# Dummy products at TensorE's waits, two queries on ScalarE and 90 instead of 87 VectorE key tiles in a planned attention layer

## The chip, the cores and the metric

The kernel runs on one core of a Trainium2 chip. Its time is device microseconds from start to end of one execution; the kernel before was run three times (347.79, 348.11 and 348.26 us; median 348.11). The core's engines are TensorE (PE in the profile; PEld are its weight loads), VectorE (DVE), ScalarE (ACT), GpSimd (POOL) and SyncE (SP), which issues most of the DMAs. Each engine runs its own list of instructions in order; semaphores hold them together.

## The reference: what is computed

A transformer layer on x of 2048 rows by 448 columns, in bf16: layer norm, attention with 16 query heads of 28 dimensions that share one key and one value head, a residual, a second layer norm, and then a routed MLP that only 8 of the 2048 rows pass through.

```
q = layernorm(x) @ wq   # 16 heads of 28
k = layernorm(x) @ wk ; v = layernorm(x) @ wv          # one head each
h = x + softmax(q k^T / sqrt(28)) v @ wo
y = layernorm(h)
r = y @ w_r ; idx = the 8 rows with the largest r
upd[idx] = (silu(y[idx] @ w_gate) * (y[idx] @ w_up)) @ w_down * sigmoid(r[idx])
out = h + y + upd
```

## The kernel before, in words

**Tiles.** The 2048 rows are 16 row tiles of 128. Attention goes by 16 query blocks (128 rows, 16 heads, so 2048 queries) against 16 key tiles of 128. For one block and one key tile TensorE makes the scores in four strips of 128x512 (`scores`, matmuls at L823). The strips' exponentials are made by one of two engines:

- an *A tile* on ScalarE: two ACTIVATE instructions of 128x1024 (L888; L874 for the early tiles below), and one group of four probability-times-value products (`pv_op`, L853, P and Vs);
- a *D tile* on VectorE: four TENSOR_SCALAR instructions of 128x512 that clip the score and use its integer bits as a bf16 number (L915, tile Y). GpSimd makes two shifted copies of the four strips with 64-bit adds (L926, tile Yc), and the three are multiplied with three differently scaled value tiles, so a D tile has three groups of products (L853, Y and Yc) where an A tile has one.

`_ND` says how many of each block's 16 key tiles are D tiles: 87 of the 256 in all. `_EARLY` names three A tiles of block 1 whose strips are made while block 0 runs; their results wait in the space of the MLP weights (`wg_sb`, `wu_sb`).

**Head.** The key and value of all rows are needed before block 0 can finish. The rows are taken in seven groups (`group`: tiles 0; 1; 2,3; 4,5; 6,7; 8 to 11; 12 to 15). A group's rows go through VectorE statistics (L724, L726), Ln and Exp on ScalarE (L728, L730), the normalization (on VectorE at L737 or L746, for tiles 1 and 2 on ScalarE at L742), TensorE transposes (L757), a VectorE copy (L762), the key product with `wk_rep` (an L628 matmul), the key's writing by VectorE (L772) and the value (L785). A key tile is kept twice, in two placings of its partitions (`K[:, 0]` and `K[:, 1]`, r = 0 and 1); strips 0 and 2 read the first, strips 1 and 3 the second. VectorE writes both, except for the groups in `_KD`, where two DMAs copy the second from the first. `q_project` makes a block's queries (16 matmuls of 128x128); VectorE adds a bias while it copies them from PSUM (L806), only the first half of block 0's is done by ScalarE (L803).

**Body.** Per block there are also a copy of the accumulator (L953), the sums' way through DRAM to their reciprocals (L959, `Rb`), the scaling (L966), the output projection `out_proj`, the residual (L996), statistics (L998, L999), the product with w_r (L1001) and, a few tiles at a time, the second norm `ln2` (L1012 to L1034).

**Tail.** For tiles 0 to 13 the best 8 rows of each are found early (`stage1`) and fetched by an indirect DMA (L1127, tile `wqx`/`cand`, norms at L1137 to L1146). `tail` then finishes block 15, norms row tile 15 (`last_rows`, L1041 to L1060), finds the best 8 of all (L1200, L1201), multiplies them with the MLP weights, fetches their rows of the output by an indirect DMA (L1256, tile `base`), adds, and writes them back (L1267).

**What sets the order.** Nothing above is emitted in the order written. Each instruction is an operation with an engine, a planned duration, reads and writes, and a priority; `_Flow.plan` is a list scheduler that places them one by one and gives every engine its fixed list. The tables `_W`, `_LOOK`, `_WIN`, `_LATE`, `_HOLD`, `TURN`, `MORE` are its rules and costs, in ns. It also gives out the PSUM banks; bank 7 (`ACC`) holds the accumulator. A lock keeps some VectorE operations and GpSimd's apart in the plan.

Of the kernel before, what the change touches and what calls it, by code (L numbers as in the profile page):

```python
# [240 lines left out]
_KD = (1, 2, 4)  # L241
_EARLY = (0, 6, 9)
# [37 lines left out]
class _Flow(_Graph):  # L280
# [7 lines left out]
    TURN = 105.0  # L288
# [225 lines left out]
def _fast(nc, G, sb, ps, psb, flag, scr, rows, A_x, A_wq, A_wk, A_wv, A_wo, B_w_r, B_w_gate, B_w_up, B_w_down, out):  # L514
# [154 lines left out]
    G.op(DV, lambda e: e.memset(idi[:, :], 1.0), 100, writes=["idi"])
# [49 lines left out]
    def group(g):  # L719
# [29 lines left out]
        for a in range(t0, t1, 2):  # L749
# [9 lines left out]
            G.op(PE, [tr(k, ch) for k in range(m) for ch in range(NCH)], m * 4 * (150 if g == 0 else 80),  # L759
                 reads=[("of", a + k) for k in range(m)] + ["ident"], writes=[u.key], take=u)  # L760
# [8 lines left out]
                  for ch in range(NCH)], 4 * (145 if g == 0 else 5 + w / 2.4), reads=[("wkr", r) for r in range(4)] + ["wk_rep"] + [("xnT", t) for t in tl_],  # L769
# [1097 lines left out]
```

## Time and profile before

| | |
|---|---|
| median of three runs | 348.11 us |
| the profiled execution | 348.56 us, its span 346.6 us |
| ScalarE busy | 325.45 us |
| VectorE busy | 319.37 us |
| TensorE busy (modelled ends) | 318.17 us |
| GpSimd busy | 190.76 us |
| ScalarE in 40 to 320 us | 280.00 of 280 us |
| VectorE in 40 to 320 us | 266.13 of 280 us |

The profiled execution's 1.96 us outside the span are not in the trace. A row of the timeline has the start, the time from the first start to the last end, the engine, the line, the operation, what it writes and reads, and how many instructions were merged (x); in brackets the idle time before it and what ended it. A row of the windows has busy time and number (x) of each engine in that stretch.

### The profile page before, as it was taken

How to read it: one execution, taken by the hardware profiler on the slowest of the kernel's cores; microseconds unless marked ns; L12 is line 12 of the kernel's file. 1: busy time of each engine (PE TensorE's matmuls, PEld its weight loads, DVE VectorE, ACT ScalarE, POOL GpSimd, SP SyncE). 2: the span in 40 equal slices, each digit the busy share in tenths (PEclk: the TensorE clock that was granted, in tenths of full speed). 3: DMA queues.
4: the chain of work that ended last, by engine and by line, in shares of the span. 5: the costliest groups of instructions: out<-in, count | busy, mean ns of one | idle time of the engine just before them, and what ended most of it. 6: DMA issues, size and time to landing. Idle time of an engine off the chain costs nothing.

```text
span 346.6 us, 8725 instructions
## 1 busy us (share of the span) xinstructions
PE 318.2 (92%) x3630; PEld 105.2 (30%) x3630; DVE 319.4 (92%) x662; ACT 325.4 (94%) x387; POOL 190.8 (55%) x206
## 2 busy tenths in 40 slices
PE   3889899999999999999999998999999999999974
PEld 2644232323232322323232322323232322222334
DVE  6998997999988999999899899999999899999874
ACT  5599999999999999999999999999999999999850
POOL 8010475666545648667456566576747456775401
PEclk9999999999999999999999999999999999999995
DMA  6510000000020205020020206020101012152210
GB/s 158 138 40 3 0 3 18 20 17 18 5 85 4 84 4 168 27 60 30 8 80 5 84 4 165 4 46 16 33 4 30 7 58 85 42 152 58 60 36 9
DMA packets 18374, 16.18 MB, mean 47 GB/s; under 512 B 6574, under 2 KB 15438, under 8 KB 18330
## 3 DMA queue, kind: packets, MB, share of 16 engines
q1 hardware_dynamic: 16826, 15.01, 15.5%
q8 instruction: 29, 0.48, 0.6%
q10 hardware_dynamic: 1392, 0.45, 0.6%
q0 software_dynamic: 112, 0.12, 0.1%
q14 instruction: 15, 0.12, 0.1%
HBM read 11.78 MB, written 3.71 MB: 45 GB/s over the span
## 4 chain that ended last, share of the span: by engine, by line
ACT 83%; DVE 9%; DMA 3%; PE 3%; issue 0%; POOLq 0%; POOL 0%; ACTq 0%; DVEq 0%
ACT P L888 80%; DVE Y L915 4%; PE ps L628 2%; DMA wqx<-in_A_wq_dram 1%; ACT wg_sb L874 1%; DMA wqx<-n_rows,cidx 1%; DVE bn L724 1%; PE ps L823 1%; DMA cidx<-gidx 1%; ACT wu_sb L874 1%; DVE K L772 0%; ACT wqx L711 0%; DVE Q L806 0%; PE ps L757 0%; DVE gidx L1123 0%
## 5 line engine op out<-in xcount | busy, mean ns | idle before, releaser
L888 ACT ACTIVATE P<-ps 128x1024 bf16<-128x1024 f32 x332 | 306.8, 1287 | 0.0
L926 POOL INT64_ADD Yc<-Y x174 | 178.5, 1037 | 127.7 <-DVE Y L915 112.3
L915 DVE TENSOR_SCALAR Y<-ps 128x512 int16<-128x512 f32 x348 | 220.0, 683 | 12.0 <-PE ps L823 11.3
L823 PE MATMUL ps<-Q,K 32*128 32x512 bf16 (+1 forms) x1024 | 147.1, 386 | 14.1 <-ACT P L888 10.8
L823 PEld LDWEIGHTS ps<-Q,K 32*128 32x128 bf16 (+1 forms) x1024 | 37.7, 91 | 142.9 <-ACT P L888 122.1
L853 PE MATMUL ps<-Yc,Vs 128*32 128x512 bf16 x696 | 63.9, 385 | 0.0
L853 PE MATMUL ps<-P,Vs 128*32 128x512 bf16 x664 | 59.4, 387 | 0.0
L853 PE MATMUL ps<-Y,Vs 128*32 128x512 bf16 x348 | 34.2, 384 | 0.2 <-DVE Ot L953 0.2
L853 PEld LDWEIGHTS ps<-P,Vs 128*32 128x32 bf16 x664 | 14.1, 93 | 28.3 <-issue 26.2
L853 PEld LDWEIGHTS ps<-Yc,Vs 128*32 128x32 bf16 x696 | 15.7, 94 | 21.5 <-issue 15.8
L628 PE MATMUL ps<-xnT,wqx 112*128 112x128 bf16 x256 | 21.6, 229 | 0.0
L628 PE MATMUL ps<-wo_pad,On 128*32 128x448 bf16 (+1 forms) x244 | 18.1, 358 | 1.2 <-DVE Y L915 0.6
L628 PEld LDWEIGHTS ps<-xnT,wqx 112*128 112x128 bf16 x256 | 15.6, 102 | 7.7 <-issue 4.8
L806 DVE TENSOR_SCALAR Q<-ps,qone 128x512 bf16<-128x512 f32 (+1 forms) x16 | 11.6, 727 | 1.0 <-PE ps L628 0.9
L853 PEld LDWEIGHTS ps<-Y,Vs 128*32 128x32 bf16 x348 | 9.1, 94 | 9.3 <-issue 7.4
L966 DVE TENSOR_TENSOR On<-Ot,Rb 128x512 bf16<-128x512 f32 x15 | 11.0, 734 | 0.5 <-DMA Rb<-l_scr 0.5
L757 PE MATMUL ps<-ident,of 128*112 128x128 bf16 x64 | 6.3, 248 | 5.5 <-DVE of L737 5.5
L996 DVE TENSOR_TENSOR of<-ps,x_sb 128x448 bf16<-128x448 f32 x15 | 9.3, 619 | 1.1 <-PE ps L628 1.1
L953 DVE COPY Ot<-ps 128x512 f32<-128x512 f32 x15 | 10.3, 685 | 0.0
L724 DVE BATCH_NORM_STATS2 bn<-x_sb 128x6 f32<-128x448 bf16 x16 | 9.5, 610 | 0.0
L998 DVE BATCH_NORM_STATS2 bn<-of 128x6 f32<-128x448 bf16 x15 | 9.3, 622 | 0.1
L1001 DVE SCALAR_TENSOR_TENSOR junk<-of,w_rb 128x448 bf16<-128x448 bf16 x14 | 8.5, 611 | 0.0
(169 smaller groups left out, 141.4 us busy)
## 6 DMA issues: line engine op xcount, KB each, us to landing
Rb<-l_scr SPq DMA_DIRECT2D x15, 256.0 KB
out_dram<-of SPq DMA_DIRECT2D x16, 112.0 KB, 2.2
n_rows<-of SPq DMA_DIRECT2D x14, 113.0 KB, 2.4
x_sb<-in_A_x_dram SPq DMA_DIRECT2D x3, 448.0 KB, 4.4
wg_sb<-in_B_w_gate_dram SPq DMA_DIRECT2D x3, 448.0 KB, 6.1
wu_sb<-in_B_w_up_dram SPq DMA_DIRECT2D x3, 448.0 KB, 6.1
xnT<-in_B_w_down_dram SPq DMA_DIRECT2D x3, 448.0 KB, 7.7
wqx<-in_A_wq_dram ACTq DMA_DIRECT2D x1, 392.0 KB, 4.6
```

Of the source, the lines that this page charges most:

```text
L628: return lambda e: e.matmul(o() if callable(o) else o, lhsT=l, rhs=r, start=start, stop=stop)
L724: G.op(DV, lambda e, t=t: e.bn_stats(bn6[:, t, :], x_sb[:, t, :]), 516, reads=[("x", t)], writes=[("bn6", t)], after=[G.last_w[("xnT", 0)] ...
L806: G.op(DV, lambda e, c=c, src=src: e.tensor_scalar(Q[:, b % 3, c[0]:c[1], :], src(), qone[:, 0:1], None, ALU.add), 60 + n * 150, reads=[u. ...
L823: return e.matmul(ps[:, u.b[0] + q, :], lhsT=K[a:a + w, i % 2, j * 128:(j + 1) * 128], rhs=Q[a:a + w, b % 3, :, :].rearrange("p h n -> p ( ...
L853: return e.matmul(ps[32 * i:32 * i + 32, ACC, :], lhsT=Vs[:, v, j, :], rhs=src(i), start=info["first"] == o.idx, stop=info["last"] == o.idx)
L888: G.op(AC, lambda e, u=u, p=p, n=n: e.activation(P[:, p:p + n, :], ps[:, u.b[0]:u.b[0] + n, :], ACT.Exp, bias=EB, scale=OCT), 50.0 + 426.5 ...
L915: G.op(DV, lambda e, u=u, g0=g0: e.tensor_scalar(Y0[:, g0, :].bitcast(I16), ps[:, u.b[0], :], 0.0, TOP - STEP[-1], ALU.max, ALU.min), 599, ...
L926: G.op(PO, lambda e: e.int64_add(Yc[:, c, :, :].rearrange("p a b -> p (a b)").bitcast(I64), Y0[:, 4 * s:4 * s + 4, :].rearrange("p a b -> ...
L953: o = G.op(DV, lambda e: e.tensor_copy(Ot[:, rb, :], ps[:, ACC, :]), 598, reads=[pk(ACC)], writes=[("Ot", rb)], prio=b - 10.0, after=blk[b ...
L966: G.op(DV, lambda e: e.tensor_tensor(On[:, rb, :, :].rearrange("p h n -> p (h n)"), Ot[:, rb, :], Rb[:, rb, :], ALU.mult), 599, reads=[("O ...
L996: G.op(DV, lambda e: e.tensor_tensor(of[:, t, 0:D], hp(), x_sb[:, t, :], ALU.add), 535, reads=[u.key, ("x", t)], writes=[("of", t)], free=u)
L998: G.op(DV, lambda e: e.bn_stats(bn6[:, t, :], of[:, t, 0:D]), 520, reads=[("of", t)], writes=[("bn6", t)])
```

## The change

It has four parts.

**Dummy products.** A helper `fill` puts products of a tile of ones with itself, 128x128x128, into the accumulator's bank, whose first real product overwrites it: 44 at the very start, 8 and 6 after the transposes of groups 0 and 1, 5 after the key product of group 0, 9 after block 0's queries. The planned durations of the first group's products are lowered (transposes 150 to 100 ns, key product 145 to 75, queries 470 and 430 to 235).

**Queries and keys of the head.** The second half of block 0's queries is copied by ScalarE too. The second placing of the keys comes by DMA for groups 3 and 5 instead of 1, 2 and 4. All three early tiles are due at the same place of block 0 (3, 3, 3 for 0, 6, 9). The two masks that GpSimd makes (`tri`, `ident`) carry a planned wait for its first 64-bit add.

**Planned times.** An exp of 128x1024 is planned at 917.4 ns for 903, a score or value group at 226 for 231, and several norm steps likewise; `TURN`, `MORE` and the weights change with them, and the plan gives a new order. `_ND` sums to 90.

**Tail.** The product with w_r of tile 14 no longer waits for its norm: it is made unscaled and multiplied by it afterwards. Tile 14's Ln is put behind the last block's reciprocals, and its two normalizations behind the Exp of tile 15's norm. The count of sums that are in range (`okc`) waits for the last product before the down projection.

```
-_KD = (1, 2, 4)
-_EARLY = (0, 6, 9)
+_KD = (3, 5)
+_EARLY = (3, 3, 3)
-_ND = (2, 7, 6, 3, 7, 7, 6, 5, 5, 7, 6, 5, 4, 5, 6, 6)
+_ND = (2, 6, 7, 4, 6, 6, 5, 7, 6, 6, 5, 6, 7, 5, 6, 6)
-_LOOK = 111.5
+_LOOK = 167.8
-    TURN = 105.0
+    TURN = 92.0
...
+    def fill(n, ns, after):
+        G.op(PE, [mm(ps[:, ACC, 0:128], idi[:, :], idi[:, :], True, True) for _ in range(n)], n * ns, reads=["idi"],
+             writes=[pk(ACC)], after=after, prio=-1999)
+
+    fill(44, 98, ())
...
+            if g == 0:
+                fill(8, 56, [o])
+            elif g == 1:
+                fill(6, 56, [o])
...
         if g == 0:
+            fill(5, 56, [G.last_w[uk.key][0]])
             q_project(0)
+            fill(9, 56, [o for o in G.ops[-8:] if o.eng == PE][-1:])
...
-            if b == 0 and c[0] == 0:
+            if b == 0:
                 G.op(AC, lambda e, c=c, src=src: e.activation(Q[:, 0, c[0]:c[1], :], src(), ACT.Identity, bias=qone[:, 0:1]),
-                     340, reads=[u.key, "qone"], writes=[("Qa", 0)], free=u)
+                     340, reads=[u.key, "qone"], writes=[("Qa" if c[0] == 0 else "Q", 0)], free=u)
...
-                                                           scale=OCT), 50.0 + 426.5 * n,
+                                                           scale=OCT), 64.0 + 426.7 * n,
...
-                G.op(DV, lambda e, t=t: e.scalar_tensor_tensor(junk[:, :], of[:, t, 0:D], st[:, t, 1:2], w_rb[:, :], ALU.mult,
-                                                               ALU.mult, accum_out=st[:, t, 4:5]), 600,
...
+        for o in late15:
+            o.deps[q.idx] = False
...
+        for o in late14:
+            o.deps[q.idx] = False
```

The orders below are what the plan made of it. The first place is TensorE's head. The names: `idi` the tile of ones, `ident,of` the transposes, `wk_rep` the key product, `wqx` the queries, `wv_sb` the value, `Q,K` score strips, `P,Vs` value products of an A tile. Before:

```order
L757 MATMUL ps<-ident,of 112x128 x4
L628 MATMUL ps<-xnT,wk_rep 128x128 x4
L628 MATMUL ps<-xnT,wqx 128x128 x16
L628 MATMUL ps<-wv_sb,xnT 128x28 x4
L757 MATMUL ps<-ident,of 112x128 x4
L823 MATMUL ps<-Q,K 128x512 x2
L628 MATMUL ps<-xnT,wk_rep 128x128 x4
L823 MATMUL ps<-Q,K 128x512 x2
```

After:

```order
L628 MATMUL ps<-idi 128x128 x44
L763 MATMUL ps<-ident,of 112x128 x4
L628 MATMUL ps<-idi 128x128 x8
L628 MATMUL ps<-xnT,wk_rep 128x128 x4
L628 MATMUL ps<-wv_sb,xnT 128x28 x4
L628 MATMUL ps<-idi 128x128 x5
L628 MATMUL ps<-xnT,wqx 128x128 x16
L628 MATMUL ps<-idi 128x128 x9
L835 MATMUL ps<-Q,K 128x512 x4
```

The dummies stand ahead of the first transposes and between the steps of group 0; the first tile's four strips follow the queries directly, ahead of group 1's transposes.

The second place is ScalarE from the queries of block 0 to the tenth exponential (`var`, `rstd` a group's norm; `of` the normalization of tile 1 or 2; `P` and `wg_sb` exponentials). Before:

```order
L742 ACTIVATE of<-x_sb,nb,rstd 128x448
L803 ACTIVATE Q<-ps,qone 128x256
L728 ACTIVATE var<-mv,ebias 128x2
L730 ACTIVATE rstd<-var 128x2
L742 ACTIVATE of<-x_sb,nb,rstd 128x448
L888 ACTIVATE P<-ps 128x1024 x2
L728 ACTIVATE var<-mv,ebias 128x2
L730 ACTIVATE rstd<-var 128x2
L728 ACTIVATE var<-mv,ebias 128x2
L730 ACTIVATE rstd<-var 128x2
L874 ACTIVATE wg_sb<-ps 128x1024 x2
L888 ACTIVATE P<-ps 128x1024 x4
```

After:

```order
L815 ACTIVATE Q<-ps,qone 128x256 x2
L734 ACTIVATE var<-mv,ebias 128x2
L748 ACTIVATE of<-x_sb,nb,rstd 128x448
L736 ACTIVATE rstd<-var 128x2
L900 ACTIVATE P<-ps 128x1024
L748 ACTIVATE of<-x_sb,nb,rstd 128x448
L900 ACTIVATE P<-ps 128x1024 x2
L734 ACTIVATE var<-mv,ebias 128x2 x2
L736 ACTIVATE rstd<-var 128x2 x2
L900 ACTIVATE P<-ps 128x1024 x5
L886 ACTIVATE wg_sb<-ps 128x1024 x2
```

Tile 1's normalization went behind the queries, tile 2's behind the first exponential, and eight exponentials of block 0 now come ahead of the first early tile.

The third place is ScalarE in the tail, from the last block's reciprocals on (`Rb` their Ln and Exp; `st` the norm of one row tile; `cst` that of the fetched rows; `xnT` and `of` a row tile's normalizations). Before:

```order
L1158 ACTIVATE Rb<-Ot 128x256
L1012 ACTIVATE st<-of,ebias 128x1
L1160 ACTIVATE Rb<-Rb 128x256
L1014 ACTIVATE st<-st 128x1
L1137 ACTIVATE cst<-wqx,ebias 112x1
L1139 ACTIVATE cst<-cst 112x1
L1026 ACTIVATE xnT<-of,st 128x448
L1030 ACTIVATE of<-of,st 128x448
L1043 ACTIVATE st<-of,ebias 128x1
L1045 ACTIVATE st<-st 128x1
L1058 ACTIVATE xnT<-ps,st 128x448
L1060 ACTIVATE of<-ps,st 128x448
```

After:

```order
L1171 ACTIVATE Rb<-Ot 128x256
L1173 ACTIVATE Rb<-Rb 128x256
L1025 ACTIVATE st<-of,ebias 128x1
L1027 ACTIVATE st<-st 128x1
L1150 ACTIVATE cst<-wqx,ebias 112x1
L1152 ACTIVATE cst<-cst 112x1
L1054 ACTIVATE st<-of,ebias 128x1
L1056 ACTIVATE st<-st 128x1
L1037 ACTIVATE xnT<-of,st 128x448
L1071 ACTIVATE xnT<-ps,st 128x448
L1073 ACTIVATE of<-ps,st 128x448
L1041 ACTIVATE of<-of,st 128x448
```

Tile 15's norm (Ln and Exp of `st`) moved ahead of tile 14's two normalizations, and stays behind the norm of the fetched rows; tile 14's output normalization is now the last of the four.

More of the change, by code (lines that the diff above doesn't have):

```diff
@@ L758, in tr @@
                                              of[:, a + k, ch * CK + cut(a, ch):(ch + 1) * CK + cut(a, ch)], ident[:, :])
-            G.op(PE, [tr(k, ch) for k in range(m) for ch in range(NCH)], m * 4 * (150 if g == 0 else 80),
-                 reads=[("of", a + k) for k in range(m)] + ["ident"], writes=[u.key], take=u)
+            o = G.op(PE, [tr(k, ch) for k in range(m) for ch in range(NCH)], m * 4 * (100 if g == 0 else 80),
+                     reads=[("of", a + k) for k in range(m)] + ["ident"], writes=[u.key], take=u)
+            if g == 0:
+                fill(8, 56, [o])
+            elif g == 1:
+                fill(6, 56, [o])
             dst = xnT[0:CK, :, a * 128:(a + m) * 128]
@@ L768, in group @@
         G.op(PE, [mm(bank(uk, c=slice(0, w)), wk_rep[0:CK, ch, :], xnT[0:CK, ch, sl], ch == 0, ch == NCH - 1)
-                  for ch in range(NCH)], 4 * (145 if g == 0 else 5 + w / 2.4), reads=[("wkr", r) for r in range(4)] + ["wk_rep"] + [("xnT", t) for t in tl_],
+                  for ch in range(NCH)], 4 * (75 if g == 0 else 5 + w / 2.4), reads=[("wkr", r) for r in range(4)] + ["wk_rep"] + [("xnT", t) for t in tl_],
              writes=[uk.key], take=uk)
@@ L832, in scores @@
             u.half = True
-        o = G.op(PE, [part(q, *p) for q, p in enumerate(parts)] if parts else strip, 231,
+        o = G.op(PE, [part(q, *p) for q, p in enumerate(parts)] if parts else strip, 226,
                  reads=[("Q", b_ % 3) for b_, j_ in need] + [("K", r, j_) for b_, j_ in need for r in range(2) if j_ not in late or r == 0] +
@@ L855, in fn @@
             return run
-        o = G.op(PE, [fn(i) for i in range(4)], 231, form="P", reads=reads + [("V", j), "Vone%d" % v], prio=key,
+        o = G.op(PE, [fn(i) for i in range(4)], 226, form="P", reads=reads + [("V", j), "Vone%d" % v], prio=key,
                  after=[blk[b - 1]["evict"] if b else None])
@@ L971, in _fast @@
     blk14 = []
+    late14 = []
+    late15 = []
     def out_proj(t):
@@ L1011, in ln2 @@
         sv = of[:, sl, D:RW].bitcast(F32)
-        G.op(AC, lambda e: e.activation(st[:, sl, 0], sv[:, :, 1], ACT.Ln, bias=ebias[:, 0:1]), 300,
-             reads=[("stf", t) for t in ts] + ["ebias"], writes=[("st0", t) for t in ts])
-        G.op(AC, lambda e: e.activation(st[:, sl, 1], st[:, sl, 0], ACT.Exp, scale=-0.5), 100, reads=[("st0", t) for t in ts],
+        ln = G.op(AC, lambda e: e.activation(st[:, sl, 0], sv[:, :, 1], ACT.Ln, bias=ebias[:, 0:1]), 175,
+                  reads=[("stf", t) for t in ts] + ["ebias"], writes=[("st0", t) for t in ts])
+        G.op(AC, lambda e: e.activation(st[:, sl, 1], st[:, sl, 0], ACT.Exp, scale=-0.5), 87, reads=[("st0", t) for t in ts],
              writes=[("st1", t) for t in ts])
@@ L1279, in tail @@
                                                                      accum_out=okc[:, n:n + 1]), dvt(w), reads=rd + ["okj"],
-                 writes=["okj", ("okc", n)], prio=900.0 if n == 0 else 1005, lock=True)
+                 writes=["okj", ("okc", n)], prio=900.0 if n == 0 else 1005, lock=True, after=[] if n == 0 else [n_])
         G.op(DV, lambda e: e.tensor_tensor(okc[:, 2:3], okc[:, 0:1], okc[:, 1:2], ALU.add), 62,
```

68 lines of the change are left out of this document (35 added, 33 removed).

## Prediction

> **What bounds the kernel now.** I read the page first: the busy line, the chain that ended last, then the costliest groups.
>
> ```profile
> PE 318.2 (92%) x3630; PEld 105.2 (30%) x3630; DVE 319.4 (92%) x662; ACT 325.4 (94%) x387; POOL 190.8 (55%) x206
> L888 ACT ACTIVATE P<-ps 128x1024 bf16<-128x1024 f32 x332 | 306.8, 1287 | 0.0
> L926 POOL INT64_ADD Yc<-Y x174 | 178.5, 1037 | 127.7 <-DVE Y L915 112.3
> L915 DVE TENSOR_SCALAR Y<-ps 128x512 int16<-128x512 f32 x348 | 220.0, 683 | 12.0 <-PE ps L823 11.3
> ```
>
> Three engines are over 90% busy, so a share over the whole run decides nothing. The windows of the body and the chain in order of time do:
>
> ```profile
> 40.00:320.00 280.00, 268.78 (x3019) 78.04 (x3020) 266.13 (x491) 280.00 (x313) 174.18 (x171) 1.00 0.16 44
> 39.66 87.16 ACT P L888 x95
> 127.99 76.15 ACT P L888 x83
> ```
>
> In the window's row the busy columns are PE, PEld, DVE, ACT, POOL. ScalarE has no idle time in 280 us; its chain pieces give a pitch of 87.16/95 = 0.9175 us for one exponential. VectorE leaves 13.87 us there. So ScalarE bounds the body, by the number of exponentials and the moment from which they run without a gap. It isn't so in the head:
>
> ```profile
> 10.95 2.06 ACT L888 ACTIVATE P<-ps 128x1024 bf16<-128x1024 f32 x2
> 16.89 1.94 ACT L874 ACTIVATE wg_sb<-ps 128x1024 bf16<-128x1024 f32 x2 [0.55 <-PE ps L823]
> 18.72 3.79 ACT L888 ACTIVATE P<-ps 128x1024 bf16<-128x1024 f32 x4
> ```
>
> Two exponentials end at 13.01, the third starts at 16.89, and the eighth ends at 22.51. From there 330 of the 338 follow (332 of L888, 6 early ones): 330 x 0.9175 = 302.8 us, with small norm steps between them, to about 326.9.
>
> **Part one: three A tiles become D tiles.** 256 - 90 = 166 A tiles are 332 exponentials, six fewer: 6 x 0.9175 = **-5.5 us** of ScalarE. VectorE gets 12 strips more. This stretch runs from VectorE's first strip to its last, for all its work and for strips alone:
>
> ```profile
> 36.65:323.13 286.48, 274.34 (x3069) 79.47 (x3065) 272.53 (x506) 286.48 (x321) 176.44 (x172) 1.00 0.16 44
> 36.65:323.13 286.48, 219.95 (x348) 1.00 0.16 44
> ```
>
> A strip takes 219.95/348 = 0.632 us there, so twelve are +7.6 us, against 286.48 - 272.53 = 13.95 us idle. The stretches in which VectorE was fullest tell more (first all its work, then strips):
>
> ```profile
> 60.00:80.00 20.00, 19.59 (x225) 5.64 (x223) 19.89 (x37) 20.00 (x23) 13.45 (x14) 1.00 0.09 27
> 220.00:240.00 20.00, 19.04 (x226) 5.29 (x222) 19.78 (x36) 20.00 (x23) 12.35 (x13) 1.00 0.12 28
> 60.00:80.00 20.00, 16.62 (x28) 1.00 0.09 27
> 220.00:240.00 20.00, 16.35 (x27) 1.00 0.12 28
> ```
>
> Here VectorE idles 0.33 of 40 us while ScalarE idles not at all, and a strip takes 32.97/55 = 0.599. Strips that follow each other closely are cheaper, because the start of one overlaps the end of the last. If all 360 ran so, they would take 215.8 us, less than the 348 now; so the twelve cost between -4.2 and +7.6 us of VectorE. TensorE gets two more groups of four products for each changed tile, six in all; GpSimd six more adds of 1.04 us, with 45% of its span free.
>
> **Part two: the head.** TensorE's first products are slow, and the same shapes are fast later:
>
> ```profile
> 0.92 0.17 DVE L669 MEMSET idi<- 128x128 bf16 x1 [0.92 <-PEq L1852]
> 7.21 1.86 PE L628 MATMUL ps<-xnT,wqx 112*128 112x128 bf16 x16
> 10.23 0.61 PE L823 MATMUL ps<-Q,K 64*128 64x512 bf16 x2 [0.56 <-DVE nb L733]
> 14.61 1.28 PE L628 MATMUL ps<-xnT,wqx 112*128 112x128 bf16 x20
> 19.95 0.39 PE L823 MATMUL ps<-Q,K 64*128 64x512 bf16 x2
> ```
>
> The sixteen query products took 1.86 us; at the rate of the twenty they would take about 1.05. A pair of strips fell from 0.61 to 0.39. The dummies keep TensorE at work from the moment the ones are there, at about 1.1 us. If group 0 then runs at the fast rate: transposes and key product save some 0.2 each (by the strips' ratio), the queries 0.8, the strips 0.2. More things of the first tile change:
>
> ```profile
> 9.19 0.60 DVE L724 BATCH_NORM_STATS2 bn<-x_sb 128x6 f32<-128x448 bf16 x1
> 9.70 0.47 DVE L806 TENSOR_SCALAR Q<-ps,qone 128x256 bf16<-128x256 f32 x1
> 1.74 1.69 POOL L697 MEMSET K<- 128x1920 bf16 x1
> 7.43 0.76 ACT L742 ACTIVATE of<-x_sb,nb,rstd 128x448 bf16<-128x448 bf16 x1 [0.23 <-DVE nb L733]
> ```
>
> The second half of the queries, whose products ended at 9.07, waited behind statistics on VectorE; on ScalarE it follows the first half at once. But tile 1's normalization, 0.76, now stands after them on ScalarE, ahead of the first exponential, and GpSimd's clearing of the keys (1.7 us) stands ahead of the masks on which VectorE's list waits, some 0.2 to 0.3. Net: the first exponential near 10.1 instead of 10.95.
>
> The larger step is the next gap. Why the third exponential came at 16.89:
>
> ```profile
> 7.66 1.15 DVE L724 BATCH_NORM_STATS2 bn<-x_sb 128x6 f32<-128x448 bf16 x2
> 11.54 0.40 DVE L772 TENSOR_SCALAR K<-ps,kcol 128x128 bf16<-128x128 f32 x1
> 11.97 1.27 SPq L640 DMA_DIRECT2D K<-K  x2
> 15.69 0.72 DVE L806 TENSOR_SCALAR Q<-ps,qone 128x512 bf16<-128x512 f32 x1
> L772 DVE TENSOR_SCALAR K<-ps,kcol x11: 381/544/810, 7.3 to 35.4; 128x256 bf16<-128x256 f32 x4, 128x512 bf16<-128x512 f32 x4, 128x128 bf16<-128x128 f32 x3
> ```
>
> Tile 1's second key placing went through two DMAs issued from 11.97 on, and the early strips that filled in waited for block 1's queries until 16.41. Now VectorE writes both placings of groups 1 and 2. I follow its new list with the durations above: statistics of two tiles 1.15, two keys 0.4 each, so tile 1's keys are there near 13.1 and its exponentials start near 14.0. Block 1's queries (0.72), the copy of tiles 2 and 3 and their keys (0.54 each, the middle one of the last row's shortest, middle and longest key) follow, and tiles 2 and 3 make the fifth to eighth exponential from 16.6 on, which ends near 20.3 instead of 22.5: **-2.2 us**. The bounds are -0.85 (the first exponential's gain alone) and -3.0 (no gap after the third). VectorE itself does 0.47 less for the queries and about 0.1 more for the keys (both placings of groups 1, 2 and 4 against 3 and 5), so it reaches its first strip only some 0.4 sooner. SyncE issues four K copies instead of six, the first of them only after group 3's keys; three early tiles, 5.5 us of exponentials, stand between the eighth exponential and tile 4, which needs them.
>
> [...]
>
> **Part three: what the new order costs ScalarE.** By itself ScalarE would gain 5.5 + 2.2 = 7.7 us. VectorE's list sets a limit. Two steps that stand ahead of its last strip now come behind it:
>
> ```profile
> 321.23 0.58 DVE L1276 TENSOR_SCALAR xnT<-Lall 128x240 f32<-128x240 f32 x1
> 321.94 0.39 DVE L1278 SCALAR_TENSOR_TENSOR xnT<-Lall,xnT 128x240 f32<-128x240 f32 x1
> ```
>
> So 36.65 - 0.4, plus 272.5, plus 7.6 at the mean price, less 1.0 for these two, is 315.4 plus idle time, against the last strip's end of 323.1 now. A gain of 7.7 leaves no idle time at the mean price and 12 us at the dense one. Midway that is 6 us in 279, about 2%, while TensorE's queue also serves ScalarE. ScalarE's new idle time is between 0 (it has none now) and 7.7 (all given back). I take **+2.2**, near the two full windows, in which both engines ran at 99% and more.
>
> **Part four: the tail.** Of the rows from the last block on, these matter:
>
> ```profile
> 330.84 0.30 ACT L1137 ACTIVATE cst<-wqx,ebias 112x1 f32<-112x1 f32 x1 [0.86 <-DMA wqx<-n_rows,cidx]
> 331.73 0.18 DVE L1042 BATCH_NORM_AGGREGATE of<-bn 128x2 f32<-128x6 f32 x1
> 332.06 0.76 ACT L1030 ACTIVATE of<-of,st 128x448 bf16<-128x448 bf16 x1
> 332.73 0.28 ACT L1043 ACTIVATE st<-of,ebias 128x1 f32<-128x1 f32 x1
> 334.47 0.72 ACT L1060 ACTIVATE of<-ps,st 128x448 bf16<-128x448 f32 x1
> 337.82 0.89 POOL L1256 DMA_INDIRECT base<-out_dram,tok  x1 [9.32 <-DVE tok L1254]
> 342.27 0.67 DVE L1264 TENSOR_TENSOR fin<-ps,base 8x256 bf16<-8x256 f32 x2 [0.30 <-PE ps L628]
> base<-out_dram,tok POOLq DMA_INDIRECT x1, 3.8
> ```
>
> Tile 15's Ln could have started at 331.9 and waited behind two normalizations until 332.73. Ahead of them it gains up to 0.8, less what the fetched rows' norm (L1137), still ahead of it, costs if those rows land late: the sign can turn, because all that follows on ScalarE waits for that DMA. But the two normalizations now come last, so the output of tile 14 is written at the time at which tile 15's was, or up to 0.5 later, and the indirect DMA at 337.82 reads all output rows; it lands 3.8 us after its issue, 0.65 before the sum that needs it. So of 0.8 about **-0.3** is left; bounds -0.8 and +0.3. The later `okc` count comes to nothing: the second half of the up products ends as the first half's down products do.
>
> **The sum.** -5.5 - 2.2 + 2.2 - 0.3 = -5.8 us. The span goes from 346.6 to 340.8, the profiled execution from 348.56 to 342.8. That execution lies 0.45 above the median of 348.11, so the median should be **342.3 us**.
>
> **The rivals.**
> 1. *VectorE becomes the bound, in part.* For it: all 13.95 us of its idle time is under 5%, and 11.3 of the 12.0 us ahead of strips is waiting for TensorE. Against: the two full windows. At the mean strip price with 2% idle (5.6 us) its last strip ends at 321.0, 2.1 sooner than now; with the tail, 345.7. From 344.6 to 347.4.
> 2. *The dummies don't bring the fast rate in time.* The 1.4 us of products return, in part hidden beside VectorE's steps: 343.4. [...]
> 3. *Slower: strips arrive as unevenly as before.* Its place is TensorE's list: strips for VectorE stand behind strips that wait for ScalarE's banks. If VectorE keeps its 13.95 us of idle time at 0.632 a strip, the last strip ends at 315.4 + 13.95 = 329.3, 6.2 us later, and the run takes 354.0 after the tail. It decides from 7.7 us of idle time on, where the last strip ends as late as now.
> 4. *Nothing moves:* the head's gain and the exponentials' are just eaten by idle time of 7.5 us on ScalarE.
>
> **How the numbers follow.** About 0.2%, 0.7 us, is what a measurement of this kernel can tell from no change (its three runs lie 0.47 apart). The forecast, with 339 to 344.6 around it for the bounds of head and tail, gets 0.60; rival 1 0.18; rival 2 0.08; rival 3 0.09; rival 4 0.05. Faster is 0.60 + 0.18 + 0.08 = 0.86, same 0.05, slower 0.09. The range from 339.0 to 347.4 leaves out rivals 3 and 4 and a little at its lower end.
>
> **What would show it.** Right: query products of about 1.1 us at 7 to 9 us; an eighth exponential that ends near 20.3; no idle time on ScalarE of more than 2 or 3 us from there on; strips at 0.60 to 0.62; the last exponential's end some 5.5 sooner. Rival 1 shows as ScalarE idle while TensorE waits for VectorE, rival 2 as sixteen queries at 1.8, rival 3 as a last strip after 323. A `cst` step that waits for its DMA with tile 15's Ln behind it would show the tail's term wrong. The forecast is wrong if the head's eighth exponential comes no sooner, or if VectorE's idle time in its strips' stretch is not well under 7.7 us at the mean price.

## The result and the profile after

The changed kernel takes 342.74 us (median of four runs, 342.41 to 343.30) against 348.02 (347.79 to 348.26): a ratio of 0.985, interval 0.9833 to 0.9867. The forecast was 342.3. The profiled execution is 342.41 us with a span of 339.8, against 348.56 and 346.6 before: the span fell by 6.8 us where 5.8 was forecast, and what lies outside it grew from 1.96 to 2.61 us.

The profile page's busy line and its two groups of exponentials and strips:

```profile
PE 322.4 (95%) x3726; PEld 113.4 (33%) x3726; DVE 322.6 (95%) x675; ACT 320.1 (94%) x382; POOL 197.0 (58%) x212
L900 ACT ACTIVATE P<-ps 128x1024 bf16<-128x1024 f32 x326 | 301.1, 1175 | 1.0 <-PE ps L835 1.0
L927 DVE TENSOR_SCALAR Y<-ps 128x512 int16<-128x512 f32 x360 | 224.4, 684 | 5.8 <-PE ps L835 5.0
```

Six exponentials fewer and twelve strips more, and VectorE's waits ahead of strips fell from 12.0 to 5.8 us. The timeline of the head, TensorE's rows first, then ScalarE's third exponential and its fifth to eighth:

```profile
1.14 4.01 PE L628 MATMUL ps<-idi 128*128 128x128 bf16 x44 [1.14 <-DVE idi L669]
7.37 1.06 PE L628 MATMUL ps<-xnT,wqx 112*128 112x128 bf16 x16
8.99 0.61 PE L835 MATMUL ps<-Q,K 64*128 64x512 bf16 x4
13.47 1.02 ACT L900 ACTIVATE P<-ps 128x1024 bf16<-128x1024 f32 x1 [0.65 <-PE ps L835]
16.50 3.77 ACT L900 ACTIVATE P<-ps 128x1024 bf16<-128x1024 f32 x4 [0.38 <-PE ps L835]
```

The sixteen query products take 1.06 us instead of 1.86, and the eighth exponential ends at 16.50 + 3.77 = 20.27 instead of 22.51. The windows (busy PE, PEld, DVE, ACT, POOL) from the fifth exponential's start at 16.50 to the end of the last one, and from VectorE's first strip to its last for all engines and for strips alone:

```profile
16.50:319.25 302.75, 295.52 (x3303) 93.99 (x3305) 295.31 (x565) 302.75 (x340) 185.39 (x181) 1.00 0.16 44
35.43:317.01 281.58, 276.27 (x3095) 84.81 (x3096) 275.62 (x512) 281.58 (x315) 182.59 (x178) 1.00 0.16 45
35.43:317.01 281.58, 224.33 (x360) 1.00 0.16 45
```

ScalarE is busy in all of its 302.75 us. VectorE idles 281.58 - 275.62 = 5.96 us where it idled 13.95, and a strip takes 224.33/360 = 0.623 us where it took 0.632. The chain that ended last, by engine, before and after:

```profile
ACT 83%; DVE 9%; DMA 3%; PE 3%; issue 0%; POOLq 0%; POOL 0%; ACTq 0%; DVEq 0%
ACT 62%; DVE 20%; PE 15%; issue 1%; POOL 0%; POOLq 0%; DVEq 0%
```

Before, this chain stays on ScalarE's exponentials until 302 us. Now it leaves them at 223.4 us and goes on along TensorE's products and VectorE's strips to the last strip, although ScalarE still has no idle time: the end of the body is no longer set by ScalarE alone. The end of the body is where before and after differ in kind. Before, the last exponentials and the first step of the tail:

```profile
317.43 9.50 ACT L888 ACTIVATE P<-ps 128x1024 bf16<-128x1024 f32 x10
327.63 0.44 DVE L1156 STREAM_SHUFFLE Ot<-ps 128x256 f32<-128x256 f32 x1
```

After, in order of time, with VectorE's last strips and GpSimd's last add:

```profile
314.40 4.87 ACT L900 ACTIVATE P<-ps 128x1024 bf16<-128x1024 f32 x5
315.18 1.91 DVE L927 TENSOR_SCALAR Y<-ps 128x512 int16<-128x512 f32 x3
319.54 1.04 POOL L938 INT64_ADD Yc<-Y  x1 [1.17 <-DVE xnT L1296]
320.62 0.63 DVE L1012 BATCH_NORM_STATS2 bn<-of 128x6 f32<-128x448 bf16 x1
320.63 0.40 PE L865 MATMUL ps<-Yc,Vs 128*32 128x512 bf16 x4 [0.21 <-POOL Yc L938]
321.17 0.44 DVE L1169 STREAM_SHUFFLE Ot<-ps 128x256 f32<-128x256 f32 x1
```

The tail began 0.70 us after the last exponential before (326.93 to 327.63) and begins 1.90 after it now (319.27 to 321.17). The last products now wait for GpSimd's copies of VectorE's last D tile, not for ScalarE. (The expectations below call this loss 1.3 us; by these rows it is 1.20.)

So the span's 6.8 us are these: 2.24 in the head (22.51 to 20.27); 5.42 from the eighth exponential to the last (304.42 to 299.00); 1.20 lost at the handover to the tail; and 0.34 from the first shuffle to the span's end (18.97 to 18.63). Outside the span 0.65 us were lost in this execution; over the four runs 2.6 to 3.4 us lie outside, against 1.9 to 2.1 for the kernel before.

### The profile page after: what moved, and what is told of

Read it like the earlier page. It is cut to its first block, busy times and chain, and to the rows that moved or that the text cites. A ratio compares the mean times of both kernels' runs of the same rounds, so it can differ in the third digit from the quotient of the medians.

```text
span 339.8 us, 8933 instructions
## 1 busy us (share of the span) xinstructions
PE 322.4 (95%) x3726; PEld 113.4 (33%) x3726; DVE 322.6 (95%) x675; ACT 320.1 (94%) x382; POOL 197.0 (58%) x212
## 4 chain that ended last, share of the span: by engine, by line
ACT 62%; DVE 20%; PE 15%; issue 1%; POOL 0%; POOLq 0%; DVEq 0%
ACT P L900 59%; DVE Y L927 12%; PE ps L835 6%; PE ps L865 5%; PE ps L628 4%; DVE bn L730 1%; ACT wg_sb L886 1%; DVE On L978 1%; DVE K L782 1%; DVE of L1010 1%; ACT wu_sb L886 1%; DVE bn L1012 1%; DVE xnT L772 0%; DVE Ot L965 0%; DVE junk L1014 0%
## 5 line engine op out<-in xcount | busy, mean ns | idle before, releaser
L900 ACT ACTIVATE P<-ps 128x1024 bf16<-128x1024 f32 x326 | 301.1, 1175 | 1.0 <-PE ps L835 1.0
L938 POOL INT64_ADD Yc<-Y x180 | 184.8, 1039 | 116.6 <-DVE Y L927 97.5
L927 DVE TENSOR_SCALAR Y<-ps 128x512 int16<-128x512 f32 x360 | 224.4, 684 | 5.8 <-PE ps L835 5.0
L835 PE MATMUL ps<-Q,K 32*128 32x512 bf16 (+1 forms) x1024 | 152.7, 385 | 4.0 <-ACT P L900 2.0
L835 PEld LDWEIGHTS ps<-Q,K 32*128 32x128 bf16 (+1 forms) x1024 | 41.2, 91 | 126.1 <-ACT P L900 93.2
L865 PE MATMUL ps<-Yc,Vs 128*32 128x512 bf16 x720 | 66.6, 384 | 0.4 <-POOL Yc L938 0.2
L865 PE MATMUL ps<-P,Vs 128*32 128x512 bf16 x652 | 62.5, 388 | 1.2 <-DVE Ot L965 0.9
L865 PEld LDWEIGHTS ps<-P,Vs 128*32 128x32 bf16 x652 | 15.6, 93 | 34.2 <-issue 31.2
L865 PEld LDWEIGHTS ps<-Yc,Vs 128*32 128x32 bf16 x720 | 16.7, 94 | 21.1 <-issue 13.6
L818 DVE TENSOR_SCALAR Q<-ps,qone 128x512 bf16<-128x512 f32 x15 | 11.2, 744 | 0.0
L782 DVE TENSOR_SCALAR K<-ps,kcol 128x256 bf16<-128x256 f32 (+2 forms) x12 | 6.3, 558 | 1.7 <-PE ps L628 1.7
```

The lines of the kernel that those rows point to most:

```text
L818: G.op(DV, lambda e, c=c, src=src: e.tensor_scalar(Q[:, b % 3, c[0]:c[1], :], src(), qone[:, 0:1], None, ALU.add), 60 + n * 150, reads=[u. ...
L835: return e.matmul(ps[:, u.b[0] + q, :], lhsT=K[a:a + w, i % 2, j * 128:(j + 1) * 128], rhs=Q[a:a + w, b % 3, :, :].rearrange("p h n -> p ( ...
L865: return e.matmul(ps[32 * i:32 * i + 32, ACC, :], lhsT=Vs[:, v, j, :], rhs=src(i), start=info["first"] == o.idx, stop=info["last"] == o.idx)
L900: G.op(AC, lambda e, u=u, p=p, n=n: e.activation(P[:, p:p + n, :], ps[:, u.b[0]:u.b[0] + n, :], ACT.Exp, bias=EB, scale=OCT), 64.0 + 426.7 ...
L927: G.op(DV, lambda e, u=u, g0=g0: e.tensor_scalar(Y0[:, g0, :].bitcast(I16), ps[:, u.b[0], :], 0.0, TOP - STEP[-1], ALU.max, ALU.min), 599, ...
L938: G.op(PO, lambda e: e.int64_add(Yc[:, c, :, :].rearrange("p a b -> p (a b)").bitcast(I64), Y0[:, 4 * s:4 * s + 4, :].rearrange("p a b -> ...
```

## The experiments

My theory after the result: the dummies and the keys' second placing carry the head's gain; six exponentials fewer carry the body's; VectorE's list decides the handover; and the new planned order is what keeps ScalarE from idling. Each of these has its rival in the runs below. All were timed beside the kernel before, which took 348.24 to 348.31 us in these sessions.

**Without the dummies.** Every other row of every engine stands as in the changed kernel.

```
     def fill(n, ns, after):
+        return
```

> The changed kernel without any dummy product; everything else, the planned durations too, stays. Theory (the dummies bring TensorE's fast rate to group 0 and that is on ScalarE's path): the sixteen query products take about 1.8 us again, the first exponential starts about 1.2 us later, the eighth ends 1.0 to 1.4 us later than 20.27, and the time is 343.7 to 344.2. Rival (the products lie beside VectorE's steps and the gain of the head comes from the keys and queries alone): the eighth exponential ends within 0.4 us of 20.27 and the time stays at 342.7 to 343.1.

Measured: 345.06 us (344.19 to 345.75; 0.9901, 0.9875 to 0.9927). TensorE's queries of block 0 and of block 1, and ScalarE's third and fifth to eighth exponential:

```profile
7.63 1.86 PE L628 MATMUL ps<-xnT,wqx 112*128 112x128 bf16 x16
12.77 1.87 PE L628 MATMUL ps<-xnT,wqx 112*128 112x128 bf16 x16
16.08 1.02 ACT L901 ACTIVATE P<-ps 128x1024 bf16<-128x1024 f32 x1 [2.67 <-PE ps L836]
19.31 3.77 ACT L901 ACTIVATE P<-ps 128x1024 bf16<-128x1024 f32 x4 [0.70 <-PE ps L836]
```

TensorE is still slow at 14 us, the third exponential waits 2.67 us, and the eighth exponential ends at 23.08, 2.8 us later than with dummies. The theory's reason held, but both ranges were too small: without dummies the change loses 2.3 us, all that the head had gained.

**Only the first 44 dummies, and only 20 at the start.** Two kernels, again with nothing else moved.

```
     def fill(n, ns, after):
+        if n != 44:
+            return
...
-    fill(44, 98, ())
+    fill(20, 98, ())
```

> Only the 44 dummies at the start are left; the 28 between the steps are gone, and nothing else moves. My theory, that the fast rate is there from 5.8 us on and waits of less than 1 us do not lose it, expects the eighth exponential's end at 20.2 to 20.5 and 342.5 to 343.1. The rival, that TensorE loses the fast rate again in the gaps between the first steps, expects matmul pairs of 0.6 somewhere before 14 us, the eighth exponential at 21 to 23 and 343.4 to 345.0.

> 20 dummies at the start for 44; the 28 between the steps stay, and nothing else moves. The first 20 end near 3.4 us, and TensorE then idles until the first transposes near 5.8. [...] The rival, that any early work brings the rate, expects what the changed kernel has: 342.5 to 343.1.

With the 44 alone: 342.76 us (342.06 to 343.02; 0.9837, 0.9819 to 0.9856), as much as with all 72. With 20 and the later 28: 343.45 (343.12 to 343.90; 0.9863, 0.9846 to 0.9879). Dummies, queries and the fifth to eighth exponential, first with the 44 alone:

```profile
1.14 4.88 PE L628 MATMUL ps<-idi 128*128 128x128 bf16 x44 [1.14 <-DVE idi L669]
7.30 1.05 PE L628 MATMUL ps<-xnT,wqx 112*128 112x128 bf16 x16
16.69 3.77 ACT L902 ACTIVATE P<-ps 128x1024 bf16<-128x1024 f32 x4 [0.37 <-PE ps L837]
```

Then with 20 at the start:

```profile
1.14 2.31 PE L628 MATMUL ps<-idi 128*128 128x128 bf16 x20 [1.14 <-DVE idi L669]
8.15 1.91 PE L628 MATMUL ps<-xnT,wqx 112*128 112x128 bf16 x16
9.85 1.11 PE L628 MATMUL ps<-idi 128*128 128x128 bf16 x9
17.64 3.77 ACT L900 ACTIVATE P<-ps 128x1024 bf16<-128x1024 f32 x4 [0.38 <-PE ps L835]
```

For the 44 the theory held: the 28 later dummies brought nothing. For the 20 the rival did not: with twenty dummies and 2.3 us of idle time behind them the fast rate was not there for group 0 (1.91 us for the sixteen query products, against 1.05). TensorE starts again at 5.8 and is slow until nearly 11 (nine dummies in 1.11 us, against 0.67 in the changed kernel), and the eighth exponential ends at 21.41.

**The second key placing by DMA again.**

```
-_KD = (3, 5)
+_KD = (1, 2, 4)
```

> The second key placing of groups 1, 2 and 4 comes by DMA again, and groups 3 and 5 are written by VectorE; the plan orders the rest anew, so that only the head, up to the eighth exponential, is to be compared. The prediction's reason (tile 1's second placing held the third exponential) expects the third exponential 1 to 3 us after 13.47 and the eighth's end at 21.0 to 22.5. The rival, that the fast products alone closed that gap, expects the eighth's end at 20.1 to 20.7.

Measured: 359.15 us (357.30 to 359.90; 1.0293, 1.0266 to 1.032). Only the head is to be compared: the key's DMAs and ScalarE's third and fourth exponential.

```profile
12.60 1.28 SPq L640 DMA_DIRECT2D K<-K  x2
17.08 1.94 ACT L900 ACTIVATE P<-ps 128x1024 bf16<-128x1024 f32 x2 [3.45 <-PE ps L835]
```

The first two exponentials start at 10.26 and 11.81 as in the changed kernel, the third at 17.08 instead of 13.47, and the eighth ends at 24.07. The gap is larger than I expected, and the DMA is only part of it. Tile 1's second placing landed at 15.04, where VectorE had both placings written at 12.89 in the changed kernel: 2.15 us. The strips then started only at 16.65, because the plan now put sixteen query products and a group's transposes ahead of them on TensorE (14.75 to 16.7). So the prediction's reason, that the DMA held tile 1, is borne out for about 2 of the 3.6 us; the rest is this kernel's order. The dummies alone do not close the gap.

**The head alone in the kernel before, 87 tiles in the changed one, and the old planned numbers with everything else new.**

```
-_KD = (1, 2, 4)
+_KD = (3, 5)
...
+    fill(44, 98, ())
```

> The kernel before with the head's part of the change alone: dummies, lowered durations of group 0, both query halves on ScalarE, key placings by DMA for groups 3 and 5, the early tiles due at one place; 87 VectorE tiles, the old planned times, rules and tail. Theory (ScalarE bounds the body without a gap, so that what the head gains is kept): the eighth exponential ends near 20.3, ScalarE has less than 1 us idle from there to the last one, and the time falls by 2.2 us to 345.8. Rival (the order of the body was found for the old head and VectorE's steps now meet it wrongly): the head gains as much and gives back at least half, 346.9 or more.

This is the kernel before with the change's dummies, queries, keys and early tiles. Measured: 350.81 us (349.24 to 353.34; 1.006, 1.0024 to 1.0096). The eighth exponential ends at 20.24, so the head gains its 2.2; then ScalarE idles 4.8 us by the brackets of its rows, and its last exponential ends at 330.76, 3.8 later than before. The rival held: a gain in the head was turned into a loss in the body. The profiled execution, 353.34 us at a mean granted clock of 0.970, is the longest of the six. The shortest, 349.24 at 0.987, a mean clock that the kernel before has too (0.984 to 0.989), is still 0.9 us above that kernel.

```
-_ND = (2, 6, 7, 4, 6, 6, 5, 7, 6, 6, 5, 6, 7, 5, 6, 6)
+_ND = (2, 7, 6, 3, 7, 7, 6, 5, 5, 7, 6, 5, 4, 5, 6, 6)
```

> The changed kernel with the block counts of before, 87 VectorE tiles. Theory (ScalarE bounds the body; three tiles are six exponentials of 0.9175 us): ScalarE's last exponential ends 5.5 us later, VectorE's idle time in the strips' stretch grows from 6 to 13 us or more, and the time is 347 to 348.5. Rival (VectorE has become the bound, so that fewer strips cost little): the time rises by less than 3 us, 343.5 to 345.7.

Measured: 347.10 us (346.22 to 347.95; 0.9962, 0.9944 to 0.998), 4.4 more than with 90 tiles. The theory held for the time and for VectorE's idle time (14.3 us); the last exponential, at 326.59, is 7.3 later and not 5.5. Six exponentials are 5.5 of this; the eighth ends 0.36 later, and ScalarE idles 1.0 us, most of it in a stretch in which TensorE ran at half clock (last section). The shuffle follows at 327.10, 0.51 after the last exponential instead of 1.90, which gives 1.4 us back.

```
-_W = {'A': -54.486, 'D': 34.257, 'C': -22.634, 'S': 52.03, 'P': 15.859, 'V': -50.352, 'G': -54.08, 'Q': -117.673, 'O':
...
+_W = {'A': -47.977, 'D': 47.993, 'C': -35.271, 'S': 57.873, 'P': 16.403, 'V': -45.666, 'G': -57.306, 'Q': -108.301,
...
-    TURN = 92.0
+    TURN = 105.0
```

> All parts of the change stay, only the planner's weights and tables (its tables of weights, windows and holds, TURN, MORE) are those of the kernel before, so that 90 tiles and the new head are planned by the old numbers. [...] The rival, that six exponentials fewer and the head decide whatever the order, expects 342.3 to 343.5 and no idle time on ScalarE.

Measured: 351.18 us (350.45 to 352.05; 1.0089, 1.0067 to 1.0111). This is the run that tells most. VectorE's stretch from its first strip to its last, its last strip, ScalarE's last exponentials and the first shuffle:

```profile
36.67:323.98 287.31, 276.79 (x3120) 86.48 (x3120) 277.30 (x519) 282.83 (x316) 182.62 (x178) 1.00 0.16 45
312.45 7.63 ACT L900 ACTIVATE P<-ps 128x1024 bf16<-128x1024 f32 x8
323.31 0.67 DVE L927 TENSOR_SCALAR Y<-ps 128x512 int16<-128x512 f32 x1
328.77 0.44 DVE L1169 STREAM_SHUFFLE Ot<-ps 128x256 f32<-128x256 f32 x1
```

The rival did not hold: the time is 7.7 us above its range. The loss is not idle time on ScalarE either, nor a lower clock of TensorE, which is 1.00 in the stretch above: from the eighth exponential on ScalarE idles 0.6 us and is done at 320.08, only 0.8 later than in the changed kernel. VectorE is 3.9 us behind it, and the tail begins 8.69 after the last exponential. Against the changed kernel VectorE's first strip starts 1.24 later, seven more steps (1.7 us) stand ahead of the last strip, and it idles 10.0 instead of 5.96: together 7.0, and its last strip ends 6.9 later. The new planned numbers are worth 8.4 us beside the same parts with the old ones.

**Three tiles more, and one moved out of the last block.**

```
-_ND = (2, 6, 7, 4, 6, 6, 5, 7, 6, 6, 5, 6, 7, 5, 6, 6)
+_ND = (2, 6, 7, 5, 6, 6, 6, 7, 6, 6, 6, 6, 7, 5, 6, 6)
```

> The changed kernel with three more VectorE tiles (blocks 3, 6, and 10 get one more), 93. If ScalarE still bounds alone, six exponentials fewer bring it to about 337.5. If VectorE has become the bound with its 6 us of idle time, twelve strips at 0.60 to 0.63 us, 7.2 to 7.6 us, use that up and more: ScalarE gets idle time of 4 us or more and the time is 342 to 346. I hold the second for likelier, since 5.96 us of 281.58 are idle on VectorE in the changed kernel's strips' stretch.

Measured: 357.38 us (356.76 to 357.76; 1.0266, 1.0247 to 1.0284), far outside my expectation. The last exponentials, the last strips and the shuffle:

```profile
318.99 2.91 ACT L900 ACTIVATE P<-ps 128x1024 bf16<-128x1024 f32 x3
326.62 2.46 DVE L927 TENSOR_SCALAR Y<-ps 128x512 int16<-128x512 f32 x4
334.72 0.44 DVE L1169 STREAM_SHUFFLE Ot<-ps 128x256 f32<-128x256 f32 x1
```

The last strip ends 7.2 us after the last exponential: with 93 tiles VectorE's list decides the end. Twelve strips are not all of that. In its strips' stretch VectorE works 283.4 us, 7.7 more, as I had expected, but it also idles 10.2 us instead of 5.96, and ScalarE waits longest at a place where its list has a norm of four row tiles, behind VectorE's statistics:

```profile
277.77 0.30 ACT L1025 ACTIVATE st<-of,ebias 128x4 f32<-128x4 f32 x1 [3.24 <-DVE of L1013]
```

From the last strip to the shuffle it takes 5.65 us instead of 4.08, and from there to the end 20.3 instead of 18.6; the granted clock was 0.50 from 329.0 to 339.3. How much each of these would cost alone, the run does not separate.

```
-_ND = (2, 6, 7, 4, 6, 6, 5, 7, 6, 6, 5, 6, 7, 5, 6, 6)
+_ND = (2, 6, 7, 5, 6, 6, 5, 7, 6, 6, 5, 6, 7, 5, 6, 5)
```

> 90 tiles, but the last block has 5 instead of 6 and block 3 has 5 instead of 4. My theory is that the 1.3 us more between the last exponential and the first shuffle are VectorE's list, which ends too late against ScalarE's: with four strips fewer at the end its last strip lies 3 us or more before the last exponential's end, the shuffle follows that end by 0.7 to 1.2, and, if block 3 has room, the time is 341.4 to 342.4. The rival is that any new order may bring back waits in the body, as it did with 87 and 93 tiles: ScalarE idles 1 us or more before the last exponential, and the time is 343.5 to 348.

Measured: 354.92 us (353.88 to 356.10; 1.0179, 1.016 to 1.0198). The rival held, and beyond its range. ScalarE waits near 276 us, and VectorE's last strip ends at 326.14, 2.15 after the last exponential:

```profile
276.48 0.30 ACT L1025 ACTIVATE st<-of,ebias 128x4 f32<-128x4 f32 x1 [1.48 <-DVE of L1013]
278.07 16.89 ACT L900 ACTIVATE P<-ps 128x1024 bf16<-128x1024 f32 x18 [1.05 <-PE ps L865]
```

The last exponential is 4.7 us later than in the changed kernel, the shuffle 8.0 and the span's end 13.7, so that the larger part of the loss lies behind the body. With the last block's load no longer the only thing that differs, this run says nothing on the handover.

**The handover.** Two kernels: the count of sums behind the tail's one-hot step, and that together with the residual of tile 14 behind the first shuffle. Only VectorE's list differs from the changed kernel's.

```
-        for n, (l, w, rd, late) in enumerate(((Lf, nL, [("L", t) for t in range(NT - 1)], ()),
+        for n, (l, w, rd, late) in enumerate(((Lf, nL, [("L", t) for t in range(NT - 1)], [G.last_w["oh"][0]]),
...
+        for o in res14:
+            for s in accr[:1]:
+                o.deps[s.idx] = False
```

> The count over the sums of blocks 0 to 14 is put behind the one-hot step of the tail, so that GpSimd's last add no longer waits for it; every other row of every engine stands as in the changed kernel. My theory is that the 1.3 us more between the last exponential and the first shuffle have two causes in a row: the add that waits for the count, and VectorE's residual and statistics of tile 14 that stand ahead of the shuffle. Then the add starts 0.5 to 1.1 us sooner, the shuffle at most 0.2 sooner, and the time is 342.5 to 343.0. The rival, that the add alone holds the tail, expects the shuffle 0.5 to 1.1 sooner and 341.6 to 342.3.

> As the run before, and the residual of tile 14 (and with it its statistics) is put behind the first shuffle of the last block; only VectorE's list differs from the changed kernel. My theory expects the first shuffle 0.3 to 0.7 us sooner, right behind the last products, at most 1.5 after the last exponential's end, and a time of 342.0 to 342.5. The rival, that the tail is then held by tile 14's norm, which comes about 0.6 later, expects 342.7 to 343.4.

Measured: 342.63 us (342.19 to 342.96; 0.984, 0.9826 to 0.9853) and 342.80 (342.43 to 343.52; 0.9848, 0.9834 to 0.9862). GpSimd's last add, the shuffle and tile 15's Ln, first with the count moved:

```profile
319.04 1.04 POOL L938 INT64_ADD Yc<-Y  x1 [0.85 <-DVE bestb L1139]
320.99 0.44 DVE L1169 STREAM_SHUFFLE Ot<-ps 128x256 f32<-128x256 f32 x1
325.19 0.29 ACT L1054 ACTIVATE st<-of,ebias 128x1 f32<-128x1 f32 x1 [0.56 <-DVE of L1053]
```

Then with the shuffle first as well:

```profile
320.62 0.44 DVE L1172 STREAM_SHUFFLE Ot<-ps 128x256 f32<-128x256 f32 x1
325.25 0.30 ACT L1057 ACTIVATE st<-of,ebias 128x1 f32<-128x1 f32 x1 [0.63 <-DVE of L1056]
```

The add starts 0.5 us sooner and the shuffle 0.18; with the shuffle first, 0.55. My theory of two causes held for the shuffle, but the rival holds for the time: tile 15's Ln comes at 325.2 either way, against 325.37. What is taken off VectorE's list ahead of the shuffle comes back behind it. So 0.55 of the 1.20 us is VectorE's work, whichever side of the shuffle it stands on. The rest was not tested: even here the shuffle comes 1.40 us after the last exponential, and GpSimd's last add still waited 0.85 us for a small step of VectorE that is kept apart from it in the plan.

**The tail's two planned waits dropped.**

```
-        for o in late15:
-            o.deps[q.idx] = False
...
-        for o in late14:
-            o.deps[q.idx] = False
```

> The two planned waits of the tail are dropped: tile 14's Ln may run between the last block's reciprocals, and its two normalizations ahead of tile 15's Ln; TensorE, GpSimd and SyncE stand as in the changed kernel. The prediction's term expects tile 15's Ln 0.3 to 0.8 later against the first shuffle and 342.9 to 343.5. The rival, that the waits bring nothing, expects 342.5 to 342.9 with the span within 0.2 of the changed kernel's.

Measured: 342.27 us (341.64 to 342.82; 0.9833, 0.9819 to 0.9846). Tile 15's Ln and the last sum in this kernel:

```profile
325.58 0.28 ACT L1054 ACTIVATE st<-of,ebias 128x1 f32<-128x1 f32 x1
335.13 0.68 DVE L1277 TENSOR_TENSOR fin<-ps,base 8x256 bf16<-8x256 f32 x2 [0.29 <-PE ps L628]
```

And in the changed kernel:

```profile
325.37 0.29 ACT L1054 ACTIVATE st<-of,ebias 128x1 f32<-128x1 f32 x1 [0.54 <-DVE of L1053]
335.13 0.67 DVE L1281 TENSOR_TENSOR fin<-ps,base 8x256 bf16<-8x256 f32 x2 [0.30 <-PE ps L628]
```

The waits put the Ln 0.21 us sooner, and the last sum starts at the same time. Neither range held (the time is lower than both, and the span 0.5 shorter), but the rival's reason did: the waits bring nothing. This version has the lowest median, but its interval overlaps that of the changed kernel.

## Why the prediction came out

**Exponentials, -5.5: right.** 5.42 us less from the eighth to the last, with ScalarE busy throughout. The run with 87 tiles agrees (4.4 us), though its order and its clock differ too.

**Head, -2.2: right in size; its steps came, but they do not add up.** The third exponential came at 13.47 where 14.0 was worked out, the eighth at 20.27 where 20.3 was. The working gave 1.4 us to faster products and most of the rest to the keys, as if they added up. But without dummies the eighth is 2.8 later, without the keys written by VectorE 3.8 (part of it by a new order), each more than the whole gain.

**Rival 2, the slow rate: did not come, and was priced for group 0 alone.** It was given 343.4. With 20 dummies TensorE was slow until nearly 11 us, through group 0, and the time was 343.45. With none it was slow until 17 us, through groups 1 and 2 as well, and the time was 345.06, which the price does not cover. How much comes also varies from execution to execution: the fast rate was there ahead of group 0's transposes, at 5.8 us, in the profiled execution of the changed kernel (0.40 us for the four), but only from 6.5 us on or later in three of the other kernels that start with the same 44 dummies (last section), where VectorE's copy of these transposes starts at 6.48 us instead of 6.30. There the eighth exponential ended at 20.46 to 20.62, 0.2 to 0.35 later.

**Rival 1, VectorE becomes the bound in part: came in its mechanism, not at its price.** The chain that ended last leaves ScalarE at 223.4 us, and VectorE's end costs 1.20 us at the handover. The sign that was named for it, ScalarE idle while TensorE waits for VectorE, did not show, and 344.6 was its lowest time: VectorE had less work than the rival took, as the next paragraph shows.

**New idle time on ScalarE, +2.2: the step that was off.** The working took half of VectorE's limit as idle time of ScalarE in the body. ScalarE idled not at all; the cost was 1.20 us, and it came at the handover, where the sum had no term. VectorE's estimate was 315.4 plus 6 us of idle time, 321.4 for its last strip; the trace has 317.09. Idle time was as estimated (5.96), but strips cost 0.623 instead of 0.632 us, its work was 275.6 instead of 272.5 + 7.6 - 1.0 = 279.1, and its first strip came at 35.43 instead of 36.25. So the last strip ends 2.2 us ahead of the last exponential. That isn't enough: from last strip to first shuffle it takes 4.08 (two adds, products, and VectorE's small steps between), from last exponential to shuffle 0.70 where ScalarE decides. VectorE's list, with GpSimd's copies behind it, is thus late by 4.08 - 2.18 - 0.70 = 1.20.

**Rival 3, strips that arrive as unevenly as before: this is the change without its new order.** It was given 354.0 and decides from 7.7 us of idle time on; with the old planned numbers VectorE idles 10.0 us, its last strip ends at 323.98, after 323, and the time is 351.2. The new numbers are why it did not come. Why just these numbers give a good order the runs do not show: five other orders, from other counts of a few tiles or from a part of the head, took 347 to 359 us.

**Tail, -0.3: right in size, wrong in reason.** The tail is 0.34 shorter, but without the two waits it is no longer than with them (18.2 us from the first shuffle to the span's end, against 18.63). In the three kernels on dummies, whose lists are the same in the tail, this stretch took 18.0, 18.3 and 18.7, so that 0.34 is hardly clear of the spread.

**Outside the span.** The sum took the 1.96 us outside the span as fixed. It grew by 0.65 to 1.4 us, and so hid that the span fell by 1.0 more than forecast. That 342.3 came so close to 342.74 is therefore in part luck: 1.0 us too much idle time was taken off the gain, and about as much came on outside the span, where nothing was forecast. In the kernels of this study the time outside the span lies between 1.8 and 3.6 us and goes with the order: 1.8 to 2.2 for the kernel before, its head alone, 87 and 93 tiles and the old numbers, 2.6 to 3.6 for the changed kernel and the runs on dummies and handover, which hold its order, the rest between. The trace does not show what it is; that stays open.

## What to carry to other kernels

Where two engines are both nearly full, compare where their lists end, with what each end still has behind it: idle time in the body shows neither. An edit that speeds up the head of a planned kernel has to be planned anew and measured with its order, for the order decided more here (8.4 us) than any of the parts. To have TensorE fast at the head, start products as soon as any data is there and keep them going until shortly before the first real ones, and read the rate from those: here 44 products from 1.14 us on, which end 0.64 us ahead of the first real ones in the changed kernel, brought sixteen query products to 1.05 and 1.06 us, from 1.86; twenty, with 2.3 us of idle time behind them, left them at 1.91, and 28 more between the steps brought nothing.

## What the runs showed of the hardware

**The fast rate comes after a time that varies.** The same 44 dummies from 1.14 us on took 4.01 us in one execution and 4.88 in the other; twenty, a gap, and products from 5.8 us on were slow until nearly 11. In the execution with 4.88 all 44 were slow, and so were the first transposes behind them (0.63 us for four, against 0.40). The windows' granted clock says 1.00 in all of these slices, so at the start the rate is read from the products and not from that column. The trace's own list of clock changes has the moment, as its first entry: 4.07 us in the changed kernel, 6.60 with the 44 alone, 10.76 with 20, 13.76 in the kernel before and 17.45 without dummies. Over the eleven profiled kernels that start with 44 dummies it lies between 3.85 and 7.15, which is 2.7 to 6.0 us after the first product. What this time depends on, the runs do not show.

**The rate can halve in the middle of the body.** Windows of 1 us in the 87-tile kernel (the number before the DMA share is the granted clock):

```profile
306.00:307.00 1.00, 0.47 (x6) 0.12 (x3) 1.00 (x3) 1.00 (x2) 0.72 (x1) 1.00 0.23 74
307.00:308.00 1.00, 1.00 (x13) 0.31 (x10) 1.00 (x3) 1.00 (x2) 1.00 (x2) 0.76 0.03 8
308.00:309.00 1.00, 1.00 (x10) 0.30 (x12) 1.00 (x2) 1.00 (x2) 0.33 (x1) 0.50 0.06 16
309.00:310.00 1.00, 1.00 (x10) 0.10 (x2) 0.38 (x2) 0.57 (x1) 0.73 (x1) 0.50 0.03 8
310.00:311.00 1.00, 1.00 (x10) 0.14 (x8) 0.96 (x2) 0.68 (x1) 1.00 (x2) 0.53 0.00 0
```

At 0.50 the clock is half; by the shares it stays there 0.48 + 1 + 1 + 0.94 = 3.42 us, and ScalarE and VectorE, both full until then, begin to idle. Worked out in the same way, the other spells of the body are 3.40 and 6.82 us (the head alone), 10.24 us (keys by DMA, from 140.5 on) and 3.42 us (five tiles in the last block): close to one, two, three and one times the 3.42 us of the first. The changed kernel's body has none. In the longest of them ScalarE was worst off:

```profile
140.00:160.00 20.00, 19.63 (x179) 5.54 (x183) 16.53 (x31) 15.42 (x17) 10.74 (x11) 0.74 0.12 33
```

It lost 4.58 of 20 us there; in the two spells of the head alone it lost 1.07 and 1.27. Spells in the body also need not come each time: the six executions of the head alone, one order, have mean clocks from 0.970 to 0.987. The spell at 307 followed slices in which TensorE was busy for 0.79, 0.86 and 0.47 of the time. But with 93 tiles slices of 0.77, 0.00 and 0.64 (from 276 on) were followed by no spell. What sets one off, and whether the planned order of the changed kernel keeps them away, is not settled by these runs.
